# Weights loaded in the order of need and converted in fewer instructions at other places: a Fourier mixing and SoLU kernel on one core

## The chip, the cores and the metric

One core of a Trainium2 chip. The metric is the time of one execution in device microseconds. The kernel before took 1401.07 us (median of 4 runs, 1398.5 to 1403.6). Several kernels were compared in one call on one chip, each beside runs of the kernel before. The "granted clock" below is the TensorE clock that the profile shows as granted, as a share of full speed.

## The reference

```python
# x: 8 x 3136 x 256, float32
X = np.fft.fft(np.fft.fft(x, axis=1), axis=2).real.reshape(25088, 256)
h  = X @ w_in                                 # 256 -> 1024
sm = softmax(h); solu = h * sm
ln = (solu - mean) / sqrt(var + 1e-6) * g_ln
out = ln @ w_out                              # 1024 -> 256
```

`w_in` and `w_out` arrive as 64-bit floats, and the kernel makes 32-bit ones of them on VectorE with integer operations.

## The kernel before

The batch is handled in four pairs. A pair's sequence is cut into eight chunks: each is loaded (`xa` on the SP queue, its mirror `xb` by a gather), added on GpSimd, folded on VectorE, transformed on PE, copied by ACT to `z` and written to memory (`zd`). Then the pair is read back turned (`turn`, five parts), and 25 units follow. A unit transforms once more, multiplies by `w_in` (`up`), does the softmax and the statistics, and transposes 32 x 32 blocks on VectorE into `v`. Sixteen DMAs per two units move these blocks from `v` to `uT` in rows of 64 floats, 256 bytes. Three units later PE multiplies by `w_out` (`down`). While the units of one pair run, the next pair's chunks are prepared between them. Only the first pair has nothing to hide behind.

```python
# [cut] pools const, xpool, zpool, gpool, qpool, small; then, behind the preparation:
fpool = ctx.enter_context(tc.tile_pool(name="fpool", bufs=2))
# [cut] conversion of one piece: 16 VectorE instructions
def narrow(c, j):
    lo, hi = raw[:, c, 2*j : 2*(j+n) : 2], raw[:, c, 2*j+1 : 2*(j+n) : 2]
    ex = tmp("ex"); bits(ex, hi, 20, ALU.logical_shift_right, 0x7FF, ALU.bitwise_and)
    # [cut] 14 more
    nc.vector.tensor_tensor(out=o[:, c, j:j+n], in0=rest, in1=top.bitcast(FP32), op=ALU.add)
# [cut] the head; all weights load at once on the ACT queue
with tc.tile_pool(name="prep", bufs=1) as prep:
    prepare = load_weights(prep)
    for step in range(1, NK):
        ahead(pairs[0], step); ahead_pe(pairs[0], step)   # chunks, then five turns
    prepare()       # w_in: 4 pieces; products with Q; w_out: 8 pieces; times g_ln; minus the mean
# [cut] the blocks of two units
self.v  = fpool.tile([P, 2, FF, 2], FP32, tag="v", bufs=2)
self.uT = fpool.tile([P, 2, KF, 4, 64], FP32, tag="uT", bufs=2)
for i in range(4):
    for q in range(4):
        nc.sync.dma_start(out=uT[b, i], in_=v[a, q])      # rows of 256 bytes
# [cut] a step of the units: up, transform of the next, join, exp, [next pair's PE work],
#       down of the unit three back, product, square, transpose, moves, stats, [next pair's loads]
```

## Time and profile before

| mark in the trace of the kernel before | us |
|---|---|
| last fold of the first pair ends | 64.6 |
| conversion of w_in, of w_out | 64.6 to 94, 94 to 132.7 |
| first `q` copied (first unit starts) | 138.8 |
| first product with w_out ends | 181.6 |
| third product with w_out ends | 205.3 |
| span | 1401.4 |

### The profile page before, as it was taken

Reading aid. Unit: us, or ns where it says so; the run is one execution under the profiler, and the core shown is the slowest. Engines: PE = TensorE matmul, PEld = TensorE weight load, DVE = VectorE, ACT = ScalarE, POOL = GpSimd, SP = SyncE. Lnnn points to the kernel's source line nnn. Section 1 sums busy time; section 2 is a strip of 40 time slices with the busy share of each in tenths; the row PEclk is TensorE's granted clock in tenths of the full one; section 3 lists DMA queues with packets and bytes.
Section 4 is the critical chain, followed back from the end, with each engine's and each line's share of the span. In section 5 each row is a group of like instructions: output and inputs, shape, how many; then the busy total and the mean of one; then the engine's idle time right before and its main releaser. Section 6 shows DMA issues by size and latency. Waiting matters only on the chain.

```text
span 1401.4 us, 15865 instructions
## 1 busy us (share of the span) xinstructions
PE 1219.9 (87%) x4864; PEld 919.1 (66%) x4864; DVE 960.7 (69%) x1481; ACT 614.0 (44%) x1149; POOL 555.8 (40%) x972
## 2 busy tenths in 40 slices
PE   1642599999998999999988999999988899998988
PEld 1311277777766667777766677777776676776667
DVE  2498877777765767777757667777765766676671
ACT  1100445545544545555544445455543544454452
POOL 3430344544354345454344335444353333332331
PEclk9566899999999989999999999999999999999998
DMA  9550469787798777877697597896888557565664
GB/s 244 185 128 0 83 120 172 146 163 136 142 165 150 132 156 136 163 159 139 130 180 141 101 167 143 149 162 129 148 157 151 90 89 134 94 107 105 110 115 92
DMA packets 464628, 189.53 MB, mean 135 GB/s; under 512 B 433206, under 2 KB 446782, under 8 KB 464288
## 3 DMA queue, kind: packets, MB, share of 16 engines
q1 hardware_dynamic: 444752, 144.45, 59.4%
q0 software_dynamic: 13824, 38.55, 10.3%
q10 hardware_dynamic: 5968, 5.52, 1.7%
q8 instruction: 40, 0.66, 0.2%
q14 instruction: 44, 0.36, 0.1%
HBM read 44.78 MB, written 38.80 MB: 60 GB/s over the span
## 4 chain that ended last, share of the span: by engine, by line
PE 64%; SPq 14%; DMA 9%; DVE 9%; issue 2%; ACT 1%; POOL 1%; POOLq 0%; DVEq 0%; ACTq 0%
PE ps_o L284 42%; PE ps_h L200 17%; SPq L278 13%; DMA out_dram<-ot 3%; DMA uT<-v 3%; DMA xa<-in_x_dram 2%; PE ps L151 2%; PE ps L174 2%; DVE ex L316 2%; DVE h L214 1%; DMA xb<-in_x_dram,idx 1%; DVE u L233 1%; ACT u L225 1%; POOL xa L120 1%; DVE v L269 1%
## 5 line engine op out<-in xcount | busy, mean ns | idle before, releaser
L284 PE MATMUL ps_o<-Wo,uT 128*128 128x256 f32 x3136 | 730.3, 393 | 75.3 <-DMA out_dram<-ot 44.1
L284 PEld LDWEIGHTS ps_o<-Wo,uT 128*128 128x128 f32 x3136 | 631.9, 203 | 153.1 <-issue 80.1
L200 PE MATMUL ps_h<-Wi,q 128*128 128x512 f32 x800 | 361.8, 595 | 8.8 <-DVE ev L206 7.3
L233 DVE SCALAR_TENSOR_TENSOR u<-h,u 128x1024 f32<-128x1024 f32 x196 | 232.5, 1223 | 139.5 <-ACT u L225 139.5
L235 POOL TENSOR_SCALAR nmean<-usum 128x1 f32<-128x1 f32 x196 | 128.6, 656 | 489.3 <-DVE u L233 489.0
L225 ACT ACTIVATE u<-h,neg 128x1024 f32<-128x1024 f32 x196 | 223.6, 1141 | 193.2 <-DVE neg L219 191.4
L242 ACT ACTIVATE h<-u,nmean 128x1024 f32<-128x1024 f32 x196 | 223.8, 1143 | 122.8 <-POOL nmean L235 122.8
L214 DVE CUSTOM_DVE_ANT_0 h<-ev,ps_h 128x1024 f32<-128x1024 f32 x196 | 231.7, 1219 | 50.3 <-PE ps_h L200 44.0
L200 PEld LDWEIGHTS ps_h<-Wi,q 128*128 128x128 f32 x800 | 152.2, 191 | 158.1 <-issue 146.5
L206 DVE SCALAR_TENSOR_TENSOR ev<-w_mid,q,ps_h 128x1024 f32<-128x1024 f32 x100 | 127.8, 1278 | 164.1 <-PE ps_h L200 158.9
L269 DVE STREAM_TRANSPOSE v<-u 128x1024 f32<-128x1024 f32 x200 | 238.8, 1236 | 0.1
L182 ACT COPY q<-ps 128x257 f32<-128x257 f32 x100 | 37.4, 374 | 250.4 <-PE ps L176 195.0
L296 POOL DMA_INDIRECT out_dram<-ot,idx x96 | 103.0, 1073 | 92.4 <-ACT ot L289 70.2
L289 ACT ACTIVATE ot<-ps_o,rs 128x256 f32<-128x256 f32 x196 | 82.9, 459 | 92.1 <-PE ps_o L284 89.1
L151 PE MATMUL ps<-y,F 98*100 98x258 f32 (+3 forms) x288 | 82.2, 427 | 44.9 <-DVE y L113 44.2
L254 POOL TENSOR_SCALAR v<-ssq 128x2 f32<-128x2 f32 (+1 forms) x100 | 26.5, 265 | 169.8 <-ACT h L242 169.8
L174 PEld LDWEIGHTS ps<-T,g 128*128 128x128 f32 x400 | 60.4, 191 | 47.4 <-issue 47.4
L151 PEld LDWEIGHTS ps<-y,F 98*100 98x100 f32 x288 | 48.7, 193 | 59.4 <-DVE y L113 25.6
L120 POOL TENSOR_TENSOR xa<-xa,xb 98x1020 f32<-98x1020 f32 (+1 forms) x32 | 72.7, 2272 | 28.6 <-DMA xa<-in_x_dram 19.9
L257 POOL TENSOR_TENSOR rs<-v,neg_half 128x2 f32<-128x2 f32 (+1 forms) x100 | 72.1, 721 | 7.8
L174 PE MATMUL ps<-T,g 128*128 128x128 f32 x400 | 60.7, 274 | 0.0
L163 POOL DMA_DIRECT2D g<-zd x80 | 47.9, 608 | 18.7 <-DMA zd<-z 11.3
(53 smaller groups left out, 492.9 us busy)
## 6 DMA issues: line engine op xcount, KB each, us to landing
uT<-v SPq DMA_DIRECT2D x784, 128.0 KB
zd<-z SPq DMA_DIRECT2D x32, 400.0 KB
g<-zd POOLq DMA_DIRECT2D x80, 160.0 KB, 5.1
out_dram<-ot SPq DMA_DIRECT2D x100, 128.0 KB
xa<-in_x_dram SPq DMA_DIRECT2D x32, 392.0 KB
raw_in_moe_w_in_dram<-in_moe_w_in_dram ACTq DMA_DIRECT2D x1, 2048.0 KB
raw_in_moe_w_out_dram<-in_moe_w_out_dram ACTq DMA_DIRECT2D x1, 2048.0 KB
uT<-v SPq DMA_DIRECT2D x32, 64.0 KB
```

Source lines behind the costliest of these rows:

```text
L151: nc.tensor.matmul(o[..., cs], F[:, 2 * t + h, :], i[..., cs], start=first, stop=True, skip_group_check=True)
L174: nc.tensor.matmul(ps[:, h * P : (h + 1) * P], g[:, k, h * P : (h + 1) * P], T[:, k1, :], start=(h == 0), stop=True, skip_group_check=True)
L200: nc.tensor.matmul(ps[:, fs], t.q[:, c * P : (c + 1) * P], Wi[:, c, fs], start=True, stop=True)
L206: nc.vector.scalar_tensor_tensor(out=t.ev, in0=w_mid, scalar=t.q[:, KD * P :], in1=ps, op0=ALU.mult, op1=ALU.add)
L214: nc.vector.tensor_tensor_reduce(out=t.h[s], in0=t.ev, in1=ps, scale=1.0, scalar=-3.0e38, op0=ALU.subtract if s else ALU.add, op1=ALU.max, ...
L225: nc.scalar.activation(out=t.u[s], in_=t.h[s], func=ACT.Exp, bias=t.neg[:, s : s + 1], accum_out=t.esum[:, s : s + 1])
L233: nc.vector.scalar_tensor_tensor(out=t.u[s], in0=t.h[s], scalar=1.0, in1=t.u[s], op0=ALU.mult, op1=ALU.mult, accum_out=t.usum[:, s : s + 1])
L235: nc.gpsimd.tensor_scalar(out=t.nmean[:, s : s + 1], in0=t.usum[:, s : s + 1], scalar1=-1.0 / FF, scalar2=None, op0=ALU.mult)
L242: nc.scalar.activation(out=t.h[s], in_=t.u[s], func=ACT.Square, bias=t.nmean[:, s : s + 1], accum_out=t.ssq[:, s : s + 1])
L269: nc.vector.transpose(out=t.batch.v[:, t.w, :, o], in_=t.u[s])
L278: nc.sync.dma_start(out=uT[b, i], in_=v[a, q])
L284: nc.tensor.matmul(ps, uT[:, c, :, s], Wo[:, c, :], start=(c == 0), stop=(c == KF - 1))
```

## The change

It shortens the conversion from 16 instructions to 8, folds g_ln into the last one, converts w_in between the folds and w_out behind units 0 and 1, puts all loads on the SP queue in the order of need, and lets the first unit start after one of the five parts of the turn.

```diff
+    fpool = ctx.enter_context(tc.tile_pool(name="fpool", bufs=2))     # earlier than before
+    g_ln, wbar, top_bit, tmp = ...                                    # now in the first pool
-            narrow: 16 instructions
+        bits(unit, hi, 20, ALU.logical_shift_right, 0x7FF, ALU.bitwise_and)
+        bits(unit, unit, -896.0, ALU.add, 0.0, ALU.max)
+        bits(unit, unit, 255.0, ALU.min, 2.0 ** 23, ALU.mult)
+        scalar_tensor_tensor(out=unit, in0=hi, scalar=top_bit, in1=unit, and, or)
+        bits(hi, hi, 0xFFFFF, ALU.bitwise_and, 0x100000, ALU.bitwise_or)
+        bits(lo, lo, 1, ALU.logical_shift_right)
+        scalar_tensor_tensor(out=m, in0=lo, scalar=2.0 ** -31, in1=hi, mult, add)
+        scalar_tensor_tensor(out=o, in0=m, scalar=scale, in1=unit, mult, mult)
+        for c in range(NC):
+            add_mirror(first, c); fold(first, c)
+            if c + 2 < NC: load(first, c + 2)
+            # [cut] two transforms of the chunk
+            if c < 3: weights.narrow_in(c + 1)
+            elif c == 3: weights.mid(); weights.load_table()
+            elif c < 7: weights.product_in(c - 4)
+            if c == NC - 2: weights.load_out()
+        weights.place_table()
+        turn(first, 0)
         # [cut] at the end of step i of the units
+            if i < 2: four pieces of weights.narrow_out
+            elif i == 2: weights.centre()          # subtraction now on GpSimd
+            if 0 < i + 1 < NK // KG: turn(first, i + 1)
```

More of the change, by code (lines that the diff above doesn't have):

```diff
@@ L83 @@
     w_mid = const.tile([P, FF], FP32, name="w_mid")
+    g_ln = const.tile([P, KF], FP32, name="g_ln")
+    wbar = const.tile([P, D], FP32, name="wbar")
+    top_bit = const.tile([P, 1], I32, name="top_bit")
     class Pair:
@@ L303, in store, with load_piece @@
             tc.add_to_no_dep_group(f"out{s}", dma.ins)
-    def load_weight(pool, w, o, engine):
+    NW = 512
+    tmp = const.tile([P, NW], I32, name="tmp")
+    def load_piece(w, raw, o, c, j, n):
         if w.dtype == FP32:
-            engine.dma_start(out=o, in_=w.rearrange("(c p) f -> p c f", p=P))
-            return lambda: None
-        raw = pool.tile([P, o.shape[1], 2 * w.shape[1]], I32, name=f"raw_{w.tensor.name}")
-        engine.dma_start(out=raw, in_=w.bitcast(I32).rearrange("(c p) f -> p c f", p=P))
-        def bits(o, i, a, op0, b=None, op1=ALU.bypass):
-            nc.vector.tensor_scalar(out=o, in0=i, scalar1=a, scalar2=b, op0=op0, op1=op1)
-        n = min(w.shape[1], 512)
-        def narrow(c, j):
-            def tmp(name, dt=I32):
-                return pool.tile([P, n], dt, tag=name, name=name)
-            lo, hi = raw[:, c, 2 * j : 2 * (j + n) : 2], raw[:, c, 2 * j + 1 : 2 * (j + n) : 2]
-            ex = tmp("ex")
-            bits(ex, hi, 20, ALU.logical_shift_right, 0x7FF, ALU.bitwise_and)
-            bits(ex, ex, -896.0, ALU.add, 0.0, ALU.max)
-            bits(ex, ex, 255.0, ALU.min)
-            bits(ex, ex, 23, ALU.logical_shift_left)
-            unit = tmp("unit")
-            bits(unit, hi, 31, ALU.logical_shift_right, 31, ALU.logical_shift_left)
-            nc.vector.tensor_tensor(out=unit, in0=unit, in1=ex, op=ALU.bitwise_or)
-            top = tmp("top")
-            bits(top, hi, 0xFFFFF, ALU.bitwise_and, 3, ALU.logical_shift_left)
-            nc.vector.tensor_tensor(out=top, in0=top, in1=unit, op=ALU.bitwise_or)
-            half, rest = tmp("ex"), tmp("rest", FP32)
-            bits(half, lo, 16, ALU.logical_shift_right, 0xFFFF, ALU.bitwise_and)
-            bits(rest, half, 2.0 ** -36, ALU.mult)
-            half = tmp("ex")
-            bits(half, lo, 0xFFFF, ALU.bitwise_and)
-            nc.vector.scalar_tensor_tensor(out=rest, in0=half, scalar=2.0 ** -52, in1=rest,
-                                           op0=ALU.mult, op1=ALU.add)
-            nc.vector.tensor_tensor(out=rest, in0=rest, in1=unit.bitcast(FP32), op=ALU.mult)
-            nc.vector.tensor_tensor(out=o[:, c, j : j + n], in0=rest, in1=top.bitcast(FP32), op=ALU.add)
-        def run():
-            for c in range(o.shape[1]):
-                for j in range(0, w.shape[1], n):
-                    narrow(c, j)
-        return run
@@ L355, in load_weights @@
-    def load_weights(pool):
-        w_in = pool.tile([P, KD, FF], FP32, name="w_in")
-        g_ln = pool.tile([P, KF], FP32, name="g_ln")
-        Q = pool.tile([P, KD, D + 1], FP32, name="Q")
-        mid = w_mid[:, 0 : KD * P].rearrange("p (c k) -> p c k", c=KD)
-        wbar = pool.tile([P, D], FP32, name="wbar")
-        narrow_in = load_weight(pool, moe_w_in, w_in, nc.scalar)
-        nc.scalar.dma_start(out=Q, in_=q_tab.rearrange("(c p) d -> p c d", p=P))
-        nc.scalar.dma_start(out=g_ln, in_=moe_g_ln.rearrange("(c p) -> p c", p=P))
-        for b in range(2):
-            nc.scalar.dma_start(out=T[b * N2 : (b + 1) * N2, :, b * N2 : (b + 1) * N2], in_=t_tab)
-        narrow_out = load_weight(pool, moe_w_out, Wo, nc.scalar)
-        def prepare():
-            narrow_in()
-            for c in range(KD):
-                nc.vector.tensor_scalar(out=mid[:, c, :], in0=ones, scalar1=Q[:, c, D:], scalar2=None, op0=ALU.mult)
-            for h in range(KD + 1):
-                ps = ps_h.tile([P, FF], FP32, tag=f"h{h % 2}", name="wps")
-                for half in range(2):
-                    fs = slice(half * HW, (half + 1) * HW)
-                    for c in range(KD):
-                        lhsT = mid[:, c, :] if h == KD else Q[:, c, h * P : (h + 1) * P]
-                        nc.tensor.matmul(ps[:, fs], lhsT, w_in[:, c, fs], start=(c == 0), stop=(c == KD - 1))
-                nc.scalar.copy(w_mid if h == KD else Wi[:, h, :], ps)
-            narrow_out()
-            for c in range(KF):
-                nc.vector.tensor_scalar(out=Wo[:, c, :], in0=Wo[:, c, :], scalar1=g_ln[:, c : c + 1],
-                                        scalar2=None, op0=ALU.mult)
@@ new lines, in load_piece, with bits, narrow @@
+            nc.sync.dma_start(out=o[:, j : j + n], in_=w.rearrange("(c p) f -> p c f", p=P)[:, c, j : j + n])
+        else:
+            src = w.bitcast(I32).rearrange("(c p) f -> p c f", p=P)
+            nc.sync.dma_start(out=raw, in_=src[:, c, 2 * j : 2 * (j + n)])
+    def bits(o, i, a, op0, b=None, op1=ALU.bypass):
+        nc.vector.tensor_scalar(out=o, in0=i, scalar1=a, scalar2=b, op0=op0, op1=op1)
+    def narrow(w, raw, o, scale):
+        n = o.shape[1]
+        if w.dtype == FP32:
+            nc.vector.tensor_scalar(out=o, in0=o, scalar1=scale, scalar2=2.0 ** 20, op0=ALU.mult, op1=ALU.mult)
+            return
+        lo, hi, unit = raw[:, 0 : 2 * n : 2], raw[:, 1 : 2 * n : 2], tmp[:, 0:n]
+        bits(unit, hi, 20, ALU.logical_shift_right, 0x7FF, ALU.bitwise_and)
+        bits(unit, unit, -896.0, ALU.add, 0.0, ALU.max)
+        bits(unit, unit, 255.0, ALU.min, 2.0 ** 23, ALU.mult)
+        nc.vector.scalar_tensor_tensor(out=unit, in0=hi, scalar=top_bit, in1=unit, op0=ALU.bitwise_and,
+                                       op1=ALU.bitwise_or)
+        bits(hi, hi, 0xFFFFF, ALU.bitwise_and, 0x100000, ALU.bitwise_or)
+        bits(lo, lo, 1, ALU.logical_shift_right)
+        m = lo.bitcast(FP32)
+        nc.vector.scalar_tensor_tensor(out=m, in0=lo, scalar=2.0 ** -31, in1=hi, op0=ALU.mult, op1=ALU.add)
+        nc.vector.scalar_tensor_tensor(out=o, in0=m, scalar=scale, in1=unit.bitcast(FP32), op0=ALU.mult,
+                                       op1=ALU.mult)
@@ new lines, with load_in, piece_in, narrow_in @@
+    class Weights:
+        def load_in(self):
+            raw = fpool.tile([P, 2, FF, 2], FP32, tag="v", name="raw_in", bufs=2)
+            raw = raw.rearrange("p a f b -> p (a f b)").bitcast(I32)
+            self.w_in = [fpool.tile([P, FF], FP32, tag="h", name="w_in", bufs=2) for _ in range(KD)]
+            self.pieces = []
+            for c in range(KD):
+                for j in range(0, FF, NW):
+                    i = 2 * (c * FF + j)
+                    self.pieces.append((moe_w_in, raw[:, i : i + 2 * NW], self.w_in[c], c, j, NW))
+        def piece_in(self, i):
+            load_piece(*self.pieces[i])
+        def narrow_in(self, i):
+            w, raw, o, c, j, n = self.pieces[i]
+            narrow(w, raw, o[:, j : j + n], 2.0 ** -20)
+        def load_tables(self):
+            self.Q = fpool.tile([P, KD, D + 1], FP32, tag="ev", name="Q", bufs=1)
+            nc.sync.dma_start(out=self.Q, in_=q_tab.rearrange("(c p) d -> p c d", p=P))
+            nc.sync.dma_start(out=g_ln, in_=moe_g_ln.rearrange("(c p) -> p c", p=P))
+        def load_table(self):
+            self.T = fpool.tile([P, NK, N2], FP32, tag="v", name="T_raw", bufs=2)
+            for b in range(2):
+                nc.sync.dma_start(out=self.T[b * N2 : (b + 1) * N2], in_=t_tab)
+        def place_table(self):
+            for b in range(2):
+                r = slice(b * N2, (b + 1) * N2)
+                nc.scalar.copy(T[r, :, r], self.T[r])
+        def mid(self):
+            self.m = w_mid[:, 0 : KD * P].rearrange("p (c k) -> p c k", c=KD)
+            for c in range(KD):
+                nc.vector.tensor_scalar(out=self.m[:, c, :], in0=ones, scalar1=self.Q[:, c, D:], scalar2=None,
+                                        op0=ALU.mult)
+        def product_in(self, h):
+            ps = ps_h.tile([P, FF], FP32, tag=f"h{h % 2}", name="wps")
+            for half in range(2):
+                fs = slice(half * HW, (half + 1) * HW)
+                for c in range(KD):
+                    lhsT = self.m[:, c, :] if h == KD else self.Q[:, c, h * P : (h + 1) * P]
+                    nc.tensor.matmul(ps[:, fs], lhsT, self.w_in[c][:, fs], start=(c == 0), stop=(c == KD - 1))
+            nc.scalar.copy(w_mid if h == KD else Wi[:, h, :], ps)
+        def load_out(self):
+            raw = fpool.tile([P, 2, KF, 4, 64], FP32, tag="uT", name="raw_out", bufs=2)
+            self.raw = raw.rearrange("p w c i m -> p (w c) (i m)").bitcast(I32)
+            self.raw = self.raw.rearrange("p (c a) m -> p c (a m)", a=2)
+            for c in range(KF):
+                load_piece(moe_w_out, self.raw[:, c], Wo[:, c], c, 0, D)
+            nc.vector.tensor_scalar(out=g_ln, in0=g_ln, scalar1=2.0 ** -20, scalar2=None, op0=ALU.mult)
+        def narrow_out(self, c):
+            narrow(moe_w_out, self.raw[:, c], Wo[:, c], g_ln[:, c : c + 1])
+        def centre(self):
@@ L390, in prepare @@
             for c in range(KF):
-                nc.vector.tensor_tensor(out=Wo[:, c, :], in0=Wo[:, c, :], in1=wbar, op=ALU.subtract)
-        return prepare
+                nc.gpsimd.tensor_tensor(out=Wo[:, c, :], in0=Wo[:, c, :], in1=wbar, op=ALU.subtract)
     def ahead(pr, step):
@@ L418 @@
         pairs = [Pair(p) for p in range(NP)]
+        first, weights = pairs[0], Weights()
         nc.sync.dma_start(out=idx, in_=mirror)
-        nc.scalar.dma_start(out=F, in_=f_tab)
-        ahead(pairs[0], 0)
+        load(first, 0)
+        nc.sync.dma_start(out=F, in_=f_tab)
+        weights.load_in()
+        weights.piece_in(0)
+        load(first, 1)
+        for i in range(1, 4):
+            weights.piece_in(i)
+        weights.load_tables()
         nc.vector.memset(ones, 1.0)
         nc.vector.memset(neg_half, -0.5)
+        bits(top_bit, neg_half[:, 0:1].bitcast(I32), 31, ALU.logical_shift_right, 31, ALU.logical_shift_left)
         nc.vector.memset(T, 0.0)
-        with tc.tile_pool(name="prep", bufs=1) as prep:
-            prepare = load_weights(prep)
-            for step in range(1, NK):
-                ahead(pairs[0], step)
-                ahead_pe(pairs[0], step)
-            prepare()
-        fpool = ctx.enter_context(tc.tile_pool(name="fpool", bufs=2))
+        weights.narrow_in(0)
+        for c in range(NC):
+            add_mirror(first, c)
+            fold(first, c)
+            if c + 2 < NC:
+                load(first, c + 2)
+            for s in range(CH // 2):
+                transform1(first, c * CH // 2 + s)
+            if c < 3:
+                weights.narrow_in(c + 1)
+            elif c == 3:
+                weights.mid()
+                weights.load_table()
+            elif c < 7:
+                weights.product_in(c - 4)
+            if c == NC - 2:
+                weights.load_out()
+        weights.place_table()
+        turn(first, 0)
         units = [Unit(p, k1) for p in range(NP) for k1 in range(NK)]
@@ L472 @@
                 stats(cur)
+            if i < 2:
+                for c in range(i * KF // 2, (i + 1) * KF // 2):
+                    weights.narrow_out(c)
+            elif i == 2:
+                weights.centre()
+            if 0 < i + 1 < NK // KG:
+                turn(first, i + 1)
             if ahd:
```

## The prediction

> **What bounds the kernel now.** I read the page's busy slices first, then a table of busy time by stage, then the instructions in order of time up to 215 us, then the chain of waits over the same stretch, and last the groups of instructions for durations. The slices of the page:
>
> ```profile
> PE   1642599999998999999988999999988899998988
> DVE  2498877777765767777757667777765766676671
> DMA  9550469787798777877697597896888557565664
> ```
>
> One slice is 35 us. PE is at 90% or more from the sixth slice on; the first five are a prologue in which something else sets the pace, and DMA stands at 0 in the fourth. My cuts by stage (PE, PEld, DVE, ACT, POOL busy, then granted clock, DMA share, GB/s):
>
> ```profile
> 0.00:65.00 65.00, 24.09 (x58) 15.05 (x59) 20.39 (x32) 9.29 (x15) 28.37 (x28) 0.76 0.85 226
> 65.00:95.00 30.00, 10.41 (x22) 5.13 (x22) 28.59 (x60) 1.17 (x2) 12.32 (x20) 0.56 0.67 160
> 95.00:133.00 38.00, 9.74 (x19) 4.11 (x18) 35.32 (x113) 3.04 (x3) 0.00 (x0) 0.63 0.00 1
> 133.00:175.00 42.00, 24.57 (x78) 14.40 (x77) 31.40 (x53) 15.62 (x29) 11.94 (x24) 0.87 0.39 69
> 175.00:215.00 40.00, 39.87 (x157) 30.71 (x158) 29.70 (x45) 19.34 (x37) 17.16 (x28) 0.93 0.74 130
> 215.00:1390.00 1175.00, 1104.43 (x4505) 843.88 (x4504) 815.26 (x1183) 564.09 (x1062) 484.07 (x871) 0.97 0.75 137
> ```
>
> Up to 65 us the loads and folds of the first pair run (DMA 0.85). From 65 to 133 VectorE alone is full (28.59 of 30, 35.32 of 38): it converts w_in, then w_out, from 64-bit words. From 133 to 175 three units run without any product with w_out. From 175 on PE is full, and stays so. In order of time, the marks between the stages are:
>
> ```profile
> 60.92 1.80 POOL L120 TENSOR_TENSOR xa<-xa,xb 98x765 f32<-98x765 f32 x1 [4.76 <-DMA xa<-in_x_dram]
> 132.67 5.56 PE L388 MATMUL cs<-Wo,ones 128*128 128x256 f32 x16 [28.26 <-DVE Wo L384]
> 138.83 0.38 ACT L182 COPY q<-ps 128x257 f32<-128x257 f32 x1 [0.18 <-PE ps L176]
> 175.13 6.49 PE L284 MATMUL ps_o<-Wo,uT 128*128 128x256 f32 x16 [8.73 <-DMA uT<-v]
> ```
>
> So everything before 175 us is a serial head, and one microsecond taken from the head is one microsecond off the end, as long as PE is still the full engine afterwards. In the chain of waits the steady state repeats about every 11.85 us per unit (186.57 to 198.42: 6.91 w_out products, 3.43 w_in products, 0.45 and 0.95 transforms), all PE; the change touches none of that.
>
> [...]
>
> ```profile
> L347 DVE TENSOR_TENSOR w_in<-rest,top 128x512 f32<-128x512 f32 x4 | 2.8, 692 | 0.1
> L347 DVE TENSOR_TENSOR Wo<-rest,top 128x256 f32<-128x256 f32 x8 | 3.4, 425 | 0.3
> L316 DVE TENSOR_SCALAR ex<-raw_in_moe_w_in_dram 128x512 int32<-128x512 int32 x12 | 5.1, 424 | 0.1
> L316 DVE TENSOR_SCALAR ex<-raw_in_moe_w_out_dram 128x256 int32<-128x256 int32 x24 | 6.9, 288 | 0.3
> ```
>
> [...] a tiny copy takes 2.76 us while GpSimd adds, and 0.30 us when it does not:
>
> ```profile
> 18.64 2.76 DVE L113 COPY y<-xa 98x8 f32<-98x8 f32 x1
> 22.60 0.30 DVE L113 COPY y<-xa 98x8 f32<-98x8 f32 x1
> ```
>
> [...] The first gather here took 11.03 us in the chain while three queues were loaded; a later load of the same size (issued 38.85, used 43.10) took 4.25. That agrees with the idea of loading in the order of need.
>
> **The change part by part.**
> (1) w_in's conversion, 64.6 to 93.96 in the chain, 29.4 us: 16 instructions on each of four pieces. It becomes 8 per piece: five single-input ones at 0.42 to 0.44 (2.1 us) and three two-input ones at 0.69 (2.1 us), 4.2 us, 17 us in all, and it moves between the folds, where VectorE is busy only 20.39 of 65 us. It leaves the path. [...]
> (2) w_out's conversion, scaling, column sum and centring, 93.96 to 141.5: off the path before the first unit, but not free. A piece of 256 columns costs five at 0.29 to 0.31 and three at 0.43, 2.75 us; four behind unit 0 and four behind unit 1 are 11 us each. In those units VectorE is itself the path.
> (3) Loads. [...] first add at about 10 us in place of 15.07. Conversion between folds 0 to 3 gives some of it back. Walking the loop (fold 1.7, load 5.5 from issue to landing, add 2.5, conversion 4.2 to 6.6 in the first four) I get folds ending near 16, 22, 30, 36, 40, 46, 50 and 57 us; before, the last ended at 64.5. The bytes needed by then (x 6.3, w_in 2, z 2.8, tables 1.3: 12.4 MB) are 218 GB/s, below the 226 that the first stage already reached.
> (4) w_in's products go between chunks 4 to 6: 8 matmuls, 3.4 us at full clock and about 7 at half. At half clock PE may be 2 us late for the last chunk.
> (5) From the last fold to the first unit. Before: 64.5 to the last copy of z at 69.2 (4.7), landing at 74.19 (5.0). One part of the turn: 4 issues of 0.575 and 5.2 to land, 7.5 (four more parts follow the first units). transform2: 1.1. So 57 + 4.7 + 5.0 + 7.5 + 1.1 + 2 (PE late) = 77.3 us for the copy of the first q, which stood at 138.83. Gain 61.5. Placing T costs ACT two copies of 1600 columns (3 us, an estimate from 0.59 for 512 and 1.01 for 1024) beside the turn.
> (6) From the first q to the end of the first w_out product. Before: 181.62 - 138.83 = 42.8 us. After, on VectorE: unit 0 10.6 (149.46 before), conversion 11, unit 1 9.85, conversion 11, unit 2 9.85: 52.3. Then the mean of the columns can be taken on ACT (0.4, behind unit 2's squares), GpSimd finishes unit 2's statistics (1.6) and subtracts on 8 tiles at 0.70 (an estimate, from 2.35 for 1020 columns and 1.80 for 765): 59.7, and the last product 0.8 later: 60.5. Loss 17.7. The moved blocks of units 0 and 1 land at 31.5 + 15.75 = 47.3, so they no longer set the start.
>
> Sum: 61.5 - 17.7 = 43.8 us; 1402 - 44 = 1358 us, 3.1% less.
>
> **The rivals.**
> A: the head becomes DMA-bound, because 2 MB of w_out, 0.8 of T and the turn meet the last loads. For it: the first stage runs at DMA 0.85. Against it: w_out is issued behind chunk 6 and needs about 9 us at 226 GB/s, so it is done before the turn. It would push the first q to 85 or 90: 1366 to 1371.
> B: the conversion of w_out takes the place of the one removed. For it: VectorE is the path in units 0 to 2. [...] Against it: GpSimd has only small statistics there.
> C: after the first product PE waits for VectorE, which is 20 us of conversions behind. Unit 3's blocks are ready about 63 us after the first q and moved at 79; PE wants them at 60.5 + 16.8 = 77. So 2 us, once; then VectorE (about 9.6 us per unit with folds) gains on PE (11.85).
> D: the old head had slack that I overrate, and the gain is larger: if w_out's conversion fits into gaps of VectorE's units, 1345.
>
> **Range and chances.** The steps err by about 6 us in the folds, 5 in the turn and 6 in the conversion, mostly one way: slower. I put 1358, range 1346 to 1374. Same at 2% means above 1374; that needs both A and B. A slower kernel would need a new stall in the steady state, for which nothing speaks. Faster 0.89, same 0.10, slower 0.01.
>
> **What would show it.** Last fold of the first pair near 57 us (50 to 63); first q near 77; w_in's converting gone from the chain; a piece of w_out near 2.75 us; first w_out product starting near 132 and released by GpSimd's subtraction, not by the blocks; from about 140 on the same 11.85 us per unit with PE at 0.95 or more. The prediction is wrong if the first q comes after 90 us, if the three units before the first product take over 70 us, or if the steady state per unit changes by over 0.15 us (15 us over 97 units).

Its sum came to 61.5 - 17.7 = 43.8 us, so 1358 us. The conversion of 4.2 to 6.6 us in the walk of (3) holds up to 2.4 us per piece for GpSimd's adds. That was an estimate of mine; what the trace shows for it is the copy of 2.76 us beside an add against 0.30 without. The first add at about 10 us was an estimate as well, which no trace had shown. Rival B has lost its size (1368). For the clocks in (4): in the kernel before, four products with w_in took 3.78 us at a granted clock of 0.50 (from 86.73 us), and eight took 3.60 at 1.00 (from 100.81).

## More of the kernel before

The prediction shows the slices and the stages. Two more lines of the page turned out to matter. They are a DMA queue (packets, MB, share of 16 engines' span) and a group of instructions (busy us, mean ns, then the idle time of the engine just before them):

```profile
q1 hardware_dynamic: 444752, 144.45, 59.4%
L284 PE MATMUL ps_o<-Wo,uT 128*128 128x256 f32 x3136 | 730.3, 393 | 75.3 <-DMA out_dram<-ot 44.1
```

PE stood still for 75.3 us in front of the w_out products. The DMA named there is a store that ended last by the profile's reckoning. The products themselves read only `uT` and `Wo`. In the built program the moves and the stores on the SP queue count on the same eight semaphores, so this view can't tell one from the other.

## The result, and the profile after

The changed kernel took 1383.8 us (median of 4 runs, 1378.4 to 1386.8) against 1401.07: 17 us less, where 44 had been predicted. The ratio is 0.9873, 95% interval 0.9834 to 0.9911. A ratio here is the mean time of one kernel's fast runs over that of the other's of the same rounds, so it is not quite the ratio of the medians.

The slices of the page after, which answer to the three of before:

```profile
PE   2644789999898899999978989999988988999998
DVE  7428866777765867777756667777765766767771
DMA  7545567765759556664676396685687345445353
```

DMA no longer stands at 0. But the prologue, where PE is under 90%, now reaches into the sixth slice, which stands at 8. My cuts by stage:

```profile
0.00:20.00 20.00, 0.28 (x1) 0.28 (x2) 11.52 (x16) 1.28 (x1) 8.64 (x11) 1.00 0.84 234
20.00:44.00 24.00, 11.74 (x26) 6.86 (x26) 23.39 (x36) 3.52 (x6) 14.39 (x11) 1.00 0.53 153
44.00:66.00 22.00, 15.84 (x45) 9.22 (x44) 7.00 (x15) 5.83 (x9) 8.21 (x7) 0.88 0.65 188
66.00:88.00 22.00, 8.50 (x33) 5.60 (x32) 0.00 (x0) 5.92 (x8) 2.44 (x4) 0.73 0.63 200
88.00:153.00 65.00, 35.09 (x89) 18.96 (x90) 52.78 (x105) 16.04 (x30) 22.07 (x40) 0.71 0.35 65
153.00:186.00 33.00, 25.86 (x102) 19.41 (x101) 21.81 (x34) 15.26 (x29) 20.61 (x35) 0.90 0.88 185
186.00:1385.00 1199.00, 1118.74 (x4574) 856.04 (x4572) 820.28 (x1191) 568.66 (x1071) 488.16 (x874) 0.96 0.61 135
```

From 20 to 44 us VectorE is full (23.39 of 24) and DMA is at 0.53. From 66 to 88 VectorE does nothing at all: it waits for the first unit. From 88 to 153 it is full again, with w_out's conversion. The marks in order of time, PE and ACT:

```profile
87.89 0.38 ACT L186 COPY q<-ps 128x257 f32<-128x257 f32 x1 [11.21 <-PE ps L180]
146.34 4.84 PE L288 MATMUL ps_o<-Wo,uT 128*128 128x256 f32 x14 [4.80 <-POOL Wo L418]
152.12 0.71 PE L288 MATMUL ps_o<-Wo,uT 128*128 128x256 f32 x2 [0.94 <-POOL Wo L418]
158.23 1.11 PE L155 MATMUL ps<-y,F 98*100 98x258 f32 x4 [1.41 <-DVE y L117]
176.93 8.78 PE L288 MATMUL ps_o<-Wo,uT 128*128 128x256 f32 x32 [5.74 <-DMA xa<-in_x_dram]
```

This gives the balance of the two profiled runs (spans of 1401.4 and 1385.0 us):

| stretch | before | after | difference | predicted |
|---|---|---|---|---|
| start to the last fold's end | 64.6 | 65.2 | +0.6 | -7.5 |
| last fold to the first q | 74.2 | 22.7 | -51.5 | -54 |
| first q to the end of the first w_out product | 42.8 | 64.9 | +22.1 | +17.7 |
| to the end of the third w_out product | 23.7 | 32.9 | +9.2 | +2, not in the sum |
| the rest | 1196.1 | 1199.3 | +3.2 | 0 |
| sum | | | -16.4 | -43.8 |

The folds gained nothing. Part of it was lost at the start: the first add came at 13.33 us, where about 10 was predicted, because the first gather still took 10.36 us (11.03 before) although the weights had left their own queue. The rest is in two views. First, in order of time, GpSimd's add and VectorE's fold at 39 us:

```profile
39.20 2.59 POOL L124 TENSOR_TENSOR xa<-xa,xb 98x1020 f32<-98x1020 f32 x1 [2.54 <-DMA xa<-in_x_dram]
39.49 2.83 DVE L115 TENSOR_TENSOR y<-xa 98x508 f32<-98x508 f32 x1
42.25 0.68 DVE L116 TENSOR_TENSOR y<-xa 98x508 f32<-98x508 f32 x1
```

The first half of the fold takes 2.83 us beside the add, the second half 0.68 alone. The conversion ahead of it has pushed the fold on top of the next chunk's add; in this trace each of the first four folds has one such stretched instruction. Conversion (4.4 us), collision (2.1) and the fold itself (1.2) make the 7.7 us per chunk. Second, the SP queue at 47 us, and the add that waits for it:

```profile
47.51 0.28 SPq L160 DMA_DIRECT2D zd<-z  x1
47.84 1.97 SPq L377 DMA_DIRECT2D T_raw<-in_t_tab_dram  x2
49.91 0.51 SPq L102 DMA_DIRECT2D xa<-in_x_dram  x1
58.04 2.33 POOL L124 TENSOR_TENSOR xa<-xa,xb 98x1020 f32<-98x1020 f32 x1 [7.19 <-DMA xa<-in_x_dram]
```

Chunk 6's buffer was free at 44.7, where fold 4 ends. Its load was issued at 49.91, behind a write of z that waited for ACT and behind T's table, and landed 8 us later. In the kernel before T and the weights had their own queue.

### The profile page after: what moved, and what is told of

It is laid out like the page before. It is cut to its first block, busy times and chain, and to the rows that moved or that the text cites. A ratio compares the mean times of both kernels' runs of the same rounds, so it can differ in the third digit from the quotient of the medians.

```text
span 1385.0 us, 15806 instructions
## 1 busy us (share of the span) xinstructions
PE 1216.1 (88%) x4864; PEld 916.4 (66%) x4864; DVE 936.8 (68%) x1395; ACT 616.5 (45%) x1151; POOL 564.5 (41%) x980
## 4 chain that ended last, share of the span: by engine, by line
PE 63%; SPq 13%; DVE 9%; DMA 8%; issue 4%; POOL 1%; ACT 1%; POOLq 0%; DVEq 0%; ACTq 0%
PE ps_o L288 41%; PE ps_h L204 18%; SPq L282 12%; DMA out_dram<-ot 4%; PE ps L155 2%; DMA uT<-v 2%; DVE h L218 2%; PE ps L178 2%; DVE u L237 2%; DVE v L273 1%; DMA xa<-in_x_dram 1%; ACT u L229 1%; DMA xb<-in_x_dram,idx 1%; DVE y L115 1%; DVE tmp L326 1%
## 5 line engine op out<-in xcount | busy, mean ns | idle before, releaser
L204 PE MATMUL ps_h<-Wi,q 128*128 128x512 f32 x800 | 366.2, 601 | 15.5 <-DVE ev L210 14.5
L155 PE MATMUL ps<-y,F 98*100 98x258 f32 (+3 forms) x288 | 78.9, 411 | 43.6 <-DVE y L117 43.6
L124 POOL TENSOR_TENSOR xa<-xa,xb 98x1020 f32<-98x1020 f32 (+1 forms) x32 | 74.2, 2319 | 27.5 <-DMA xa<-in_x_dram 17.4
L158 ACT COPY z<-ps 100x512 f32<-100x512 f32 x64 | 36.4, 569 | 50.7 <-PE ps L155 50.7
```

Of the source, the lines that this page charges most:

```text
L155: nc.tensor.matmul(o[..., cs], F[:, 2 * t + h, :], i[..., cs], start=first, stop=True, skip_group_check=True)
L204: nc.tensor.matmul(ps[:, fs], t.q[:, c * P : (c + 1) * P], Wi[:, c, fs], start=True, stop=True)
```

## The experiments

Times are medians of 4 runs, ratios are against the kernel before. The changed kernel's ratio is 0.9873 (0.9834 to 0.9911). It was run at another time. A difference of a few microseconds to it is mostly within these intervals.

**d1_cheap_out** (one copy of a piece instead of its eight conversion instructions):

```diff
-            narrow(moe_w_out, self.raw[:, c], Wo[:, c], g_ln[:, c : c + 1])
+            nc.vector.tensor_copy(out=Wo[:, c], in_=self.raw[:, c, 0:D])
```

> The changed kernel with one copy of 256 columns in place of the eight conversion instructions of each w_out piece (wrong result on purpose; loads, column sum and subtraction stay). Theory 'w_out's conversion sits on the path of units 0 to 2': units 1 and 2 each come about 10.7 us earlier (12.1 - 4 x 0.35), the first w_out product ends near 131 us in place of 152.7, and the time falls by 17 to 22 us against the changed kernel, to 1362 to 1367. Rival 'the moved blocks and the parts of the turn set the first products': under 8 us, above 1376.

Measured: 1367.2 us, ratio 0.9776 (0.9710 to 0.9841). The first w_out product ended at 134.4 in place of 152.8. By the medians the conversion in units 0 and 1 cost 17 us, by the ratios 14. That is the predicted order (17.7), so that step was nearly right; its 22.1 came from small terms: pieces of 3.02 us and not 2.75 (two of a piece's eight instructions read a scalar per partition and took 0.48, while the third one of two inputs, with a constant, took 0.43), the first unit with w_in's products at 5.27 us in place of 3.71, and 6.5 us of subtraction where 5.6 was reckoned.

**d2_cheap_in**:

```diff
-            narrow(w, raw, o[:, j : j + n], 2.0 ** -20)
+            nc.vector.tensor_copy(out=o[:, j : j + n], in_=raw[:, 0:n])
```

> The changed kernel with one copy of 512 columns in place of the eight conversion instructions of each w_in piece (wrong result on purpose). Theory 'conversion between the folds and its collisions with GpSimd's adds pace chunks 0 to 3 (7.7 us each)': the last fold ends 7 to 12 us earlier than 65.2, and the time falls by as much, to 1372 to 1377. Rival 'bytes bound the head': the last fold moves by less than 3 us, the time stays within 3 us of 1384.

Measured: 1385.4 us, ratio 0.9888. The sixth fold ended at 44.1 in place of 50.8, but the seventh at 60.0, and the last at 61.8. The theory's 7 to 12 us were there up to chunk 5 and then lost: chunk 6's load was issued at 42.4 and added at 54.7. So the conversions pace the first chunks, and behind them stands a second wait, for the loads. Neither theory alone holds, and the time did not fall.

**d3_T_last**:

```diff
             elif c == 3:
                 weights.mid()
-                weights.load_table()
+            if c == NC - 3:
+                weights.load_table()
```

> The changed kernel with the load of T's table issued behind the last load of x and not ahead of chunk 6's. Theory 'chunk 6 waits in the one queue behind T': the load of chunk 6 is issued near 47.9 in place of 49.9, lands about 5 us later in place of 8, the last fold ends near 60 in place of 65.2, and the time falls by 4 to 6 us, to 1378 to 1380. Rival 'bandwidth': the last fold within 2 us of 65.2, the time within 2 us of 1384.

Measured: 1385.0 us, ratio 0.9895. Chunk 6 was folded at 58.7 in place of 63.4, as the theory says. Then chunk 7 took the wait over (issued 51.7, added at 62.2), and the last fold ended at 65.9. The first q still came 4.3 us earlier (83.6), as PE was done with chunk 6 and w_in's third product sooner. The time did not follow (1378 to 1380 had been expected).

**d4_spread_turns**:

```diff
-            if 0 < i + 1 < NK // KG:
-                turn(first, i + 1)
+            if i % KG == 1 and i < NK - KG:
+                turn(first, i // KG + 1)
```

> The changed kernel with parts 1 to 4 of the turn issued one every five units (at units 1, 6, 11 and 16) and not one behind each of units 0 to 3. Theory 'the parts of the turn hold up GpSimd's adds and the moved blocks': the wait of 5.7 us before the third w_out product falls below 2, the transform of pair 1 no longer waits 1.4 us, the time falls by 4 to 7 us, to 1377 to 1380. Rival 'VectorE, late by its conversions, makes the blocks late': the wait stays above 4 us and the time within 2 us of 1384.

Measured: 1392.0 us, ratio 0.9942: by the medians 8 us slower than the changed kernel, with intervals that overlap (0.9875 to 1.0008), where 4 to 7 us of gain were expected. The transform of pair 1 no longer waited, but the wait before the third product was still 4.5 us, and from that product's end (184.2) to the end of the span it took 1208 us, where d1 to d3 took 1203 (and the changed kernel 1199). It may be that the parts of the turn were better off early, while PE was idle anyway, and that the steady units have no slack for extra transfers. This run alone does not show it.

**d5_before_short**, the kernel before with the short conversion alone:

```diff
+    top_bit = const.tile([P, 1], I32, name="top_bit")
-            narrow: 16 instructions; then Wo times g_ln
+            narrow: the 8 instructions of the change; g_ln in the last one
```

> The kernel before with only the conversion shortened (8 instructions a piece, g_ln folded into the last one); order of loads, place of the conversions and the turn as before. Theory 'both conversions lie whole on the path of the kernel before': w_in's falls from 29.4 to 4 x 4.3 = 17 us, w_out's with its scaling from 38.7 to 8 x 2.95 = 24, together 27 us less, 1374, which would be more than the whole change gained. Rival 'something else (the turn, the lead-in) waits behind them anyway': over 1390.

Measured: 1300.6 us, ratio 0.9257 (0.9206 to 0.9309). The first q came at 107.5, 31 us earlier, near the 27 expected. But the time fell by 104. From the third product on PE had lost most of its waits, while packets and bytes were the same as before:

```profile
q1 hardware_dynamic: 444752, 144.45, 43.8%
L285 PE MATMUL ps_o<-Wo,uT 128*128 128x256 f32 x3136 | 709.6, 385 | 24.9 <-DMA uT<-v 14.5
```

Nothing in the edit touches the units, except that the new small tile stands in the first pool and moves every later buffer. In the built programs the addresses of `v` and `uT`, modulo 256 bytes, are 224 in the kernel before, 32 in the changed one, and 0 here. The runs f1 to f4 and h1, h2 test that.

**e0_early_loads**:

```diff
-                weights.load_table()             # chunk 3
-            if c == NC - 2: weights.load_out()
+            if c == 0: weights.load_table()
+            if 0 < c < 4: weights.load_out(three pieces)
```

> The changed kernel with T's table and w_out loaded in chunks 0 to 3, where the DMA share is 0.53, in place of chunks 3 and 6. Theory 'the loads of T and w_out hold up chunks 6 and 7 and the last write of z': the last fold ends at 58 to 61 in place of 65.2, the first q comes at 78 to 82 in place of 87.9, and the time falls by 6 to 9 us, to 1375 to 1378. Rival 'what the head gains here the units give back in waits for moved blocks, as in the two runs before': the first q earlier, the time within 3 us of 1384.

Measured: 1379.9 us, ratio 0.9827 (0.9775 to 0.9879). The first q came at 81.6, as expected. The last fold ended at 64.4, not at 58 to 61. So most of the gain of 6 us came behind the last fold. From there to the last copy of z it took 4.0 us in place of 8.5, since chunk 6 was folded at 59.9 in place of 63.4 and PE was done with w_in's third product sooner; z's last write, with w_out no longer loading beside it, took 5.6 in place of 7.3. By the medians 4 us reached the end, between the two theories, but the intervals overlap.

**e1_hidden**:

```diff
+            for k in {4: (0, 1), 5: (2, 3), 6: (4,), 7: (5, 6, 7)}.get(c, ()):
+                weights.narrow_out(k)            # with the loads of e0; centre on VectorE, before unit 0
-            if i < 2: four pieces of weights.narrow_out   # units 0 and 1
```

> The same early loads, with w_out converted between the folds of chunks 4 to 7 and centred on VectorE before the first unit; w_in's third product behind chunk 5. Theory: no conversion is left in units 0 to 2, the first w_out product starts 36 to 38 us behind the first q (as before: 36.3), near 118 to 122, and the time is 1354 to 1362. Rival 'the folds of chunks 4 to 7 are pushed back by the conversions': the first q at 88 or later, the time over 1366.

Measured: 1359.6 us, ratio 0.9678 (0.9624 to 0.9733), in the expected range. The parts did not come as expected: the first q came at 87.2, since these conversions pushed the last fold to 70.3, and the first product started at 131.8, 44.6 us behind it and not 36 to 38. The rival was right on the fold, not on the time.

**e2_split_first**:

```diff
-                if last:
+                if last or i < 2:
                     move_blocks(batch, slice(cur.w, cur.w + 1))
```

> The same with the blocks of units 0 and 1 moved unit by unit and not as one batch. Theory 'the first product waits for both units' blocks': it starts 27 to 30 us behind the first q in place of 36 to 38, and the time falls by 3 to 6 us against the kernel without the split. Rival 'the blocks of units 2 and 3 set the pace anyway': the first product earlier, the time within 2 us.

Measured: 1362.7 us, ratio 0.9682. The first product started at 117.4, 31 us behind the first q (86.2), near the expected 27 to 30, but the third one ended at 160.4 against 161.4. The time did not fall (by the medians it is 3 us longer, and its runs spread from 1354 to 1371), so the theory's gain is absent; that the later blocks set the pace, as the rival has it, fits the third product's end.

**f1_before_at0, f2_after_at0, f3_before_at32, f4_after_at224**: nothing but unused bytes ahead of the unit buffers (32, 224, 64 and 192). By the built programs all unit buffers behind them shift by as much, also those of VectorE and ACT and `ot`, which the stores read.

```diff
+    pad_pool = ctx.enter_context(tc.tile_pool(name="pad_pool", bufs=1))
+    pad_pool.tile([P, 8], FP32, name="pad")
     fpool = ctx.enter_context(tc.tile_pool(name="fpool", bufs=2))
```

> The kernel before with nothing changed but 32 unused bytes ahead of the unit buffers, so that the blocks' rows of 256 bytes (buffers v and uT) start at a multiple of 256 and not 224 bytes past one. Theory 'the start of the rows sets the cost of moving blocks, and the moves, not PE, set the pace of the units': the head stays (first q near 139), the waits of PE for blocks (about 65 us behind 200 us) fall to about 20, and the time falls by 60 to 75 us, to 1327 to 1342. Rival 'the short conversion itself changed the units' pace in the run before': within 5 us of 1401.

> The changed kernel with 224 unused bytes ahead of the unit buffers, so that the rows start at a multiple of 256 and not 32 past one. Theory of the rows' start: the time falls by 60 to 80 us, to 1304 to 1324, and the change is then worth its head gain, 17 to 25 us against the kernel before with the same start. Rival: within 5 us of 1384.

> The kernel before with 64 unused bytes ahead of the unit buffers, so that the rows start 32 bytes past a multiple of 256, as in the changed kernel. Theory 'the change's gain came from its head[...]': within 6 us of 1401, and the packets' share of the queue near 50%. Rival 'the change gained by moving the rows' start from 224 to 32': 10 to 18 us faster than the kernel before.

> The changed kernel with 192 unused bytes ahead of the unit buffers, so that the rows start 224 bytes past a multiple of 256, as in the kernel before. Theory as in the run above: within 6 us of 1384, packets' share near 59%. Rival: 10 to 18 us slower than the changed kernel.

Measured (medians in us, ratios in brackets), by the start of the rows modulo 256:

| kernel | 0 | 32 | 224 |
|---|---|---|---|
| before | 1323.5 (0.9463) | 1403.4 (1.0011) | 1400.1 (1) |
| changed | 1308.0 (0.9352) | 1383.8 (0.9873) | 1389.9 (0.9934) |
| difference | 15.5 | 19.6 | 10.2 |

f1 fell by 77 us, a little more than expected, and f2's gain against f1 is a little under the 17 to 25 expected. For f1 the page has, against 59.4% and 75.3 us of waits above:

```profile
q1 hardware_dynamic: 444752, 144.45, 42.6%
L284 PE MATMUL ps_o<-Wo,uT 128*128 128x256 f32 x3136 | 706.0, 384 | 20.7 <-DMA uT<-v 12.2
```

The waits of PE fell from 75.3 to 20.7 us with 32 unused bytes. A cut of the steady units from 210 to 1250 us, first the kernel before, then f1:

```profile
210.00:1250.00 1040.00, 979.69 (x4013) 747.22 (x4012) 733.92 (x1071) 506.60 (x954) 442.78 (x789) 0.97 0.77 141
```

```profile
210.00:1250.00 1040.00, 1021.12 (x4265) 783.37 (x4264) 780.91 (x1135) 536.29 (x1014) 466.58 (x835) 0.99 0.57 147
```

In the same 1040 us f1 did 4265 matmuls where the kernel before did 4013: 6% more. DMA's share fell from 0.77 to 0.57 though more was moved (147 against 141 GB/s). The compute instructions, whose buffers shifted too, did not get faster: a transpose took 1237 and 1235 ns, an exponential 1141 in both, and a product 379 at the median. So the shift acts through the transfers. That a move then takes longer than the slack of three units is argued, as the trace has no landing times for the moves. A wait can cost again: in the changed kernel the 32 products at 176.93, behind a wait of 5.7 us, took 8.78 us at a granted clock of 0.81, and those at 159.34 took 6.91 at 1.00. Not every wait does: in d1 32 products behind 3.1 us took 7.15.

Two things follow. The change keeps a gain where most waits of PE are gone: f2 is 15 to 16 us, 1.2%, under f1, and each of the two ratios has an interval of about 5 us to either side. And the row start moved by the change, from 224 to 32, helped little: before at 32 is not faster (f3). The changed kernel at 224 is 6 us slower than at 32 by the medians, with intervals that just overlap (0.9895 to 0.9973 against 0.9834 to 0.9911), so a few microseconds of the 17 may be due to that. The packets' share did go down for 32, to 47.5% in f3:

```profile
q1 hardware_dynamic: 444752, 144.45, 47.5%
```

By this share (share x 16 x span / packets, an estimate) a packet took 20.2, 24.0 and 29.9 ns in the kernel before at 0, 32 and 224. The times do not follow: 1323.5, 1403.4 and 1400.1 us. So a packet's time alone does not give the kernel's. Nor do three starts show that it is 256, and not a smaller number, that counts.

**h1_uT_at0, h2_v_at0**: the kernel before with `uT` (written), and with `v` (read), at a multiple of 256, by 32 bytes between them, and by 32 ahead of and 224 between them. By the built programs h2 moves `v` alone. h1 moves `uT` and every unit buffer behind it, `ot` among them.

> The kernel before with 32 unused bytes between the two buffers of the moves: uT (written) starts at a multiple of 256, v (read) 224 past one. If the write side carries the cost: 1323 to 1335. If the read side does: 1390 to 1405. If each carries a part: between.

> The kernel before with v (read) at a multiple of 256 and uT (written) 224 past one. If the read side carries the cost: 1323 to 1335; if the write side: 1390 to 1405; if each a part: between, and the two gains add up to about 77 us.

Measured: 1381.1 us (ratio 0.9873) and 1379.1 us (0.9858). Each side alone gives 18 to 20 us, both 77. "Each a part" is right, but the parts do not add up to 77: mending the second side gives more than the first. The packets' share does not add up either: 59.4% before, 57.7 in h1, 55.7 in h2, 42.6 in f1. By the same estimate h1's packets took 28.6 ns where f3's took 24.0, in a kernel 22 us faster. Why is not settled. Nor is the part of `uT` told from that of `ot`: no run moves one without the other. The stores are the smaller suspect, with 25,088 rows against 409,600 of the moves.

**g1_hidden_at0**: e1 with rows at a multiple of 256.

> The kernel with early loads and w_out converted in chunks 4 to 7 (1359.6 us with rows 32 past a multiple of 256), now with rows at a multiple of 256. Theory 'w_out's conversion in units 0 to 2 cost the change 20 us': 20 to 26 us under the changed kernel with aligned rows (1308), 1282 to 1288. Rival 'once the moves are cheap, VectorE catches up and the conversions there cost little': over 1298.

Measured: 1286.4 us, ratio 0.9206 (0.9184 to 0.9229), as expected, 22 us under the changed kernel at the same row start (f2). It was run at another time.

**g2_best_at0**:

```diff
-            for k in {4: (0, 1), 5: (2, 3), 6: (4,), 7: (5, 6, 7)}.get(c, ()):
+            for k in {5: (0,), 6: (1,), 7: range(2, KF)}.get(c, ()):
+            if i == 0: weights.centre()          # on GpSimd, as in the change
```

> The same with only one piece of w_out behind chunks 5 and 6 each, six behind the last fold, and the subtraction on GpSimd in unit 0. Theory 'the conversions between folds 5 to 7 pushed the last fold from 64.4 to 70.3': the first q at 82 to 84 in place of 87, the time 3 to 5 us under the kernel before it in this call. Rival 'VectorE then comes late to unit 0': within 2 us of it.

Measured: 1283.6 us, ratio 0.9166 (0.9141 to 0.9192), by the medians the fastest correct kernel and 8% under the kernel before. Some 5% of that is the row start (f1, 0.9463), and it is 1% under d5 (0.9257), which only shortens the conversion and has the same row start. The first q came at 83.6, as expected, and the last fold ended at 67.8. Its interval and g1's just overlap, and 2.8 us lie between the theory's 3 to 5 and the rival's 2, so this comparison settles nothing. The first product of the changed kernel at row start 0 and of g2:

```profile
144.18 5.13 PE L290 MATMUL ps_o<-Wo,uT 128*128 128x256 f32 x14 [4.43 <-POOL Wo L420]
```

```profile
127.81 6.42 PE L290 MATMUL ps_o<-Wo,uT 128*128 128x256 f32 x16 [10.19 <-DMA uT<-v]
```

In the changed kernel the subtraction releases the product, 59 us behind its first q (84.99). In g2 it is the moved blocks, 44 us behind.

## Why the prediction was right or wrong

The mechanism, serial work taken off the head, was right. What failed were two terms of the sum: the folds, which were to end 7.5 us earlier and ended 0.6 later, and the waits behind the first w_out product, which the sum left out and which took 9.2 us.

- **The conversions leave the path before the first unit.** Right: from the last fold to the first q 51.5 us were gained, 54 predicted.
- **"I get folds ending near 16, 22, 30, 36, 40, 46, 50 and 57 us."** Wrong by 8.2 us, one of the two largest misses. The folds ended at 19.7, 27.4, 35.3, 43.0, 44.7, 50.8, 63.4 and 65.2. Three terms were mis-sized. The first fold was already 3.7 us late, by the gather. From the first to the fourth fold each step took 7.7 to 7.9 us, where the walk had 6, 8 and 6: an add held up VectorE in every one. The walk had allowed for adds that stretch the conversion (up to 2.4 us per piece); in this trace the instructions stretched beside an add were those of the folds, a half to 2.83 us. In f4, whose head is the same code, they were conversions too (512 columns in 2.71 us in place of 0.69), and the last fold ended at 65.0 all the same. And chunk 6's load was given 5.5 us from the fold before it, but took 13 (5.2 to be issued behind z and T, 8 to land). d2 takes the conversion away and d3 the table ahead of chunk 6: then chunk 6's load, or chunk 7's, sets the last fold.
- **Turn and first q at 77.3.** The turn took 5.2 us from its first issue to the last landing (7.5 predicted), z's last write 7.3 in place of 5.0, and PE's w_in product between the last transforms put 8.5 us between the last fold and the last copy of z, where 4.7 + 2 were reckoned. Together 2.4 us too few.
- **w_out's conversion in units 0 to 2: loss of 17.7.** Nearly right: 22.1 in the trace, 14 to 17 by d1. Its release was named rightly: GpSimd's subtraction.
- **Rival C, "2 us, once".** Mis-sized: 9.2 us, and left out of the sum. It is 1.4 for a transform behind GpSimd's queue, 5.7 in front of the third product (the view names a load of `xa`, but the products read only `uT` and `Wo`, so it was taken for the blocks of units 2 and 3), and 1.9 for the products behind that wait at a lower clock (0.81). d4 shows that the parts of the turn are not the main cause; with rows at 0 the wait of 5.7 is still 3.4. What makes these blocks late is not shown.
- **"All PE; the change touches none of that."** Its second half held: the rest changed by 3 us. Its first half fell. I took 11.85 us per unit from the chain at 186 to 198 us, where no wait stood. The mean from the first product to the end was (1401.4 - 181.6) / 97 = 12.6 us. For f1 the same division gives (1319.1 - 176.6) / 97 = 11.8, so the difference goes with the start of the rows. The division was to be had before; I did not make it.
- **Where the 44 us went**: 8.2 to the folds, 2.4 behind them, 4.4 to longer units 0 to 2, 9.2 to the waits behind them, 3.2 to the rest: 27.4 of 43.8.
- **What was not asked:** whether the short conversion alone would do. d5's ratio over f1's, both at row start 0, is 0.9257 / 0.9463 = 0.978, 29 us (23 by the medians), more than the whole change at that start (0.9352 / 0.9463 = 0.988). They were run at other times. Other buffers lie 32 bytes off in d5. The first q agrees: 107.5 in d5, 137.0 in f1. At the same row start the changed kernel (f2, first q at 85.0) starts its units 22 us sooner still than d5, and loses more than that afterwards.

## What to carry to other kernels

Work that is moved off a serial stretch has to land where its engine is idle: here VectorE was empty for 22 us in front of the first unit, while the conversions were put behind it, on the path; g1 moved them ahead and gained 22 us. Before trusting a rate read from one clean period of a steady stage, divide the stage's time by its count, and ask for the waits. And where rows as short as the 256 bytes here are moved in a steady stage, look at the addresses of their buffers in the built program before comparing two kernels, since 32 bytes added elsewhere were worth 77 us here (f1), where the change under test was worth 17.
